# A gated mix of a state-space convolution and a mixer MLP on one core: the first mixer layer regrouped into three tiles of 128 channels and one of 64, with the gate's sums and some weight splits on other engines

## The chip, the cores and the metric

One core of a Trainium2 chip runs the whole program. The metric is the device time of one execution in microseconds (us): the median of three runs of the kernel before is 380.18 us (380.03 to 381.19). One further execution was recorded by the profiler; its own time is 380.4 us and its span, from the first to the last recorded instruction, is 378.6 us.

## What is computed

The reference mixes two branches of the same input x (2048 tokens, 448 channels). With L = 2048, D = 448, N = 256, F = 1792:

```python
x = A_u
g = _sigmoid((x * gate_w).sum(-1, keepdims=True))
a = _A_ref(x, ...)            # diagonal state-space convolution over L, plus u * D_skip
b = _B_ref(x, w1, w2, w3, w4)
return g * a + (1 - g) * b

def _B_ref(x, w1, w2, w3, w4):
    h = _gelu(_layernorm(x, axis=-1) @ w1)        # 448 -> 448, the first layer
    c = D // 4                                    # four channel groups of 112
    g0 = h[:, :, 0*c:1*c] shifted by +1 token     # (padded with zeros at the ends)
    g1 = h[:, :, 1*c:2*c] shifted by -1
    g2 = h[:, :, 2*c:3*c] shifted by +2
    g3 = h[:, :, 3*c:   ] shifted by -2
    hs = concatenate([g0, g1, g2, g3], -1) @ w2   # 448 -> 448, the second layer
    x1 = x + hs
    h2 = _gelu(_layernorm(x1, axis=-1) @ w3) @ w4 # 448 -> 1792 -> 448
    return x1 + h2
```

## The kernel before

**Precision.** Every float32 operand of a large matmul is split in two: a high part that TensorE takes exactly (type fp32r, written by ScalarE with a Copy) and a low part, the difference, written by VectorE. A product is then high·high + low·high + high·low: three matmuls for each tile. The input has 448 = 3·128 + 64 channels; the low part of the last 64 is stacked under their high part (`split_lo`, L360 to L365), so the contraction takes 4 + 4 + 3 = 11 matmuls of 512 columns for each output tile.

**Units.** The work of the mixer goes in units, `("a", b, i)` and then `("d", b, f)`. b is one of four blocks of 512 tokens. An a-unit is one channel group i of 112 of the first layer and its share of the second; the four groups are taken in the order 0, 2, 1, 3, so that unit n = 4b + 1 is group 2. A d-unit is one of 14 tiles of 128 of the 1792 hidden channels. There are 16 a-units (n = 0 to 15) and 56 d-units.

**One a-unit.** `first(n)` (L419, matmuls in L437) multiplies the block, read at the shifted token offset, by w1 (11 matmuls into one PSUM bank). `act_mul` (L440, VectorE) multiplies by the tokens' reciprocal standard deviations, which lie along the free axis in the row tile rb; they come from VectorE's and ScalarE's statistics, a Newton iteration (`rstd`, on VectorE in block 0 and 1, on GpSimd later: two instructions on VectorE, then 12 on GpSimd, L323 to L326), a TensorE transpose and a ScalarE copy (`rstd_rows`, L333). `act_head` (L448, ScalarE) applies the gelu (L456), `act_copy` (L466, ScalarE) writes the high part uh (L468), `act_tail` (L470, VectorE) the low part ul (L472), and `second(n)` (L482) multiplies uh and ul by w2: 3 products x 4 token tiles = 12 matmuls of 448 columns (L499). After a block's last group the sums are added to xs (L505).

**The order** is written by hand. `begin` (L805) lists block 0 by itself, with the splits of w1 and w2, the statistics and the warm-up matmuls. After that, one pass n of the main loop issues: work listed under `before` and `after` for n, `act_tail(n+1)`, `first(n+2)`, work under `between`, `act_head(n+2)`, `act_copy(n+2)`, `second(n)`. Each engine takes its instructions in that order, and waits at the front of its queue. The lists (`at(n, fn, ...)`, L905 on) hold the statistics, the splits of later inputs and weights (`split_xt`, `sp3`, `sp4`), the layer norm of the second stage (`norm_d`, `norm_turn`, `norm_hi`, `norm_lo`) and the convolution (`ssm_...`).

**The gate's logits** come from TensorE: the weight tiles of groups 0 and 1 have 114 columns, the last two of which hold gate_w, so two rows of the first layer's output are x·gate_w. `logits` (L537) copies them out with ScalarE (five times an instruction of 18 partitions x 512), a DMA writes them to memory, `logits_in` reads them back, and `gates` (L552) transposes them on TensorE and applies the sigmoid.

Names in the rows: p is the first layer's PSUM tile, rb the row of reciprocals, uf the scaled and then gelu'd tile, uh and ul its high and low parts, acc the second layer's sums, raw an input as loaded, xh and xl its parts, w1h/w1l to w4h/w4l the weights' parts. Lines of kernel.py:

Of the kernel before, what the change touches and what calls it, by code (L numbers as in the profile page):

```python
# [8 lines left out]
F32 = mybir.dt.float32  # L9
# [3 lines left out]
OP = mybir.AluOpType  # L13
# [11 lines left out]
GW = G + 2  # L25
# [4 lines left out]
SHIFT = (1, -1, 2, -2)  # L30
EPS = 1e-5
# [14 lines left out]
def gated_mix_kernel(tc, x, xT, xb, x0, w1, w2, w3, w4, par, logdt, dskip, ident, parg, uflip, lags, out):  # L46
    nc = tc.nc
    with tc.tile_pool(name="keep", bufs=1) as keep:
# [3 lines left out]
        with ExitStack() as ctx:  # L52
            mixer_and_small_steps(ctx, tc, xs, gg, okm, x, xT, xb, x0, w1, w2, w3, w4, par, logdt, dskip, ident, out)
# [121 lines left out]
def mixer_and_small_steps(ctx, tc, xs, gg, okm, x, xT, xb, x0, w1, w2, w3, w4, par, logdt, dskip, ident, out):  # L175
# [16 lines left out]
    lg = dr.tile([1, L + 2], F32, name="lg")  # L192
# [16 lines left out]
    nu = big.tile([128, 4, 4], F32, name="nu")  # L209

# [30 lines left out]

    w1h, w1l = wpair([128, 4, 4, GW], "w1")
    w2h, w2l = wpair([G, 4, D], "w2")
    w1r = big.tile([128, 4, 4, GW], F32, name="w1r", tag="w4al")
    w2r = big.tile([128, 4, D], F32, name="w2r", tag="w4ah")

    def first_loads():
# [5 lines left out]
        act(w1r[:, 0], w1[:, 0])  # L253
        sp(r[:, :2 * HW], x0[:, :2 * HW])
        act(w1r[:, 2], w1[:, 2])
# [3 lines left out]
        sp(w1r[:, 1], w1[:, 1])  # L259
# [3 lines left out]
        sp(w1r[:, 3], w1[:, 3])  # L263
# [6 lines left out]
    def constants():  # L270
# [7 lines left out]
        nc.gpsimd.memset(carry, 0.0)  # L278
        nc.gpsimd.memset(rb[:, 0:HALO], 0.0)
# [139 lines left out]
    def first(n, bank="p1", seq=None, stop=True):  # L419
# [3 lines left out]
        if kind == "a":  # L423
            m = GW if i < 2 else G
            wh, wl = w1h[:, i, :, :m], w1l[:, i, :, :m]
            o = HALO - SHIFT[i]
        else:
            m = 128
            wh, wl = (w[:, :, i * m:(i + 1) * m] for w in (w3h, w3l))
            o = 0  # L430
# [4 lines left out]
        every = [(w, x_, k, 0, TB) for w, x_, r in ((0, 0, 4), (1, 0, 4), (0, 1, 3)) for k in range(r)]  # L435
        for q, (w, x_, k, t0, t1) in enumerate(seq or every):
            nc.tensor.matmul(p[:m, t0:t1], (wl if w else wh)[:, k, :], (xl if x_ else xh)[:, k, o + t0:o + t1],  # L437
                             start=(q == 0 and fresh), stop=stop if q + 1 == len(seq or every) else False)

    def act_mul(n):  # L440

        kind, b, i = units[n]
        m = G if kind == "a" else 128
        UF[n] = wk.tile([128, TB], F32, name="uf")
        o = b * TB + HALO - SHIFT[i]
        nc.vector.tensor_mul(UF[n][:m], P1[n][:m], rb[:m, o:o + TB])  # L446

    def act_head(n, later=False):  # L448
        kind, b, i = units[n]
        m = G if kind == "a" else 128  # L450
# [597 lines left out]
```

## Time and profile before

| | |
|---|---|
| median of three runs | 380.18 us |
| profiled execution, own time | 380.4 us |
| its span | 378.6 us |
| TensorE busy | 368.5 us, 1713 matmuls |
| VectorE busy | 295.8 us |
| ScalarE busy | 210.2 us |
| GpSimd busy | 71.1 us |

A profile's page gives the busy time of each engine, the chain that ended last and the groups of instructions. In the rows PE is TensorE, DVE VectorE, ACT ScalarE, POOL GpSimd. A row of a timeline has the start, the duration, engine, line, operation, output<-inputs, shape, count and, in brackets, how long the engine had been idle and what released it. Instructions of an engine overlap a little: two 512-column operations of VectorE start 0.60 us apart and each lasts 0.69 us.

### The profile page before, as it was taken

Reading aid. Unit: us, or ns where it says so; the run is one execution under the profiler, and the core shown is the slowest. Engines: PE = TensorE matmul, PEld = TensorE weight load, DVE = VectorE, ACT = ScalarE, POOL = GpSimd, SP = SyncE. Lnnn points to the kernel's source line nnn. Section 1 sums busy time; section 2 is a strip of 40 time slices with the busy share of each in tenths; the row PEclk is TensorE's granted clock in tenths of the full one; section 3 lists DMA queues with packets and bytes.
Section 4 is the critical chain, followed back from the end, with each engine's and each line's share of the span. In section 5 each row is a group of like instructions: output and inputs, shape, how many; then the busy total and the mean of one; then the engine's idle time right before and its main releaser. Section 6 shows DMA issues by size and latency. Waiting matters only on the chain.

```text
span 378.6 us, 5180 instructions
## 1 busy us (share of the span) xinstructions
PE 368.5 (97%) x1713; PEld 314.6 (83%) x1713; DVE 295.8 (78%) x527; ACT 210.2 (56%) x349; POOL 71.1 (19%) x187
## 2 busy tenths in 40 slices
PE   7998999999999999999999999999999999999993
PEld 4786888888888888888888888888888888888883
DVE  4888979785858981998399989999787999996312
ACT  4764646546978467643465575465756654442220
POOL 3200070322000000040023536324041440000000
PEclk9999999999999999999999999999999999999998
DMA  8970606166615219000843515256685311372202
GB/s 266 397 265 1 224 1 173 30 118 209 209 56 157 46 50 214 3 0 12 243 72 78 83 29 153 63 160 124 97 183 134 78 28 19 73 189 48 77 0 102
DMA packets 85896, 42.26 MB, mean 112 GB/s; under 512 B 67030, under 2 KB 80614, under 8 KB 85226
## 3 DMA queue, kind: packets, MB, share of 16 engines
q1 hardware_dynamic: 85434, 41.20, 41.6%
q10 hardware_dynamic: 432, 0.70, 0.6%
q8 instruction: 15, 0.25, 0.3%
q14 instruction: 15, 0.12, 0.1%
HBM read 30.86 MB, written 11.02 MB: 111 GB/s over the span
## 4 chain that ended last, share of the span: by engine, by line
PE 90%; DVE 3%; ACT 2%; DMA 2%; issue 1%; POOL 0%; SPq 0%; DVEq 0%
PE p L437 46%; PE acc L499 43%; DMA w1r<-w_in 2%; PE acc L520 1%; ACT uh L468 1%; ACT uf L456 1%; PE misc L336 0%; DVE uf L446 0%; DVE z L638 0%; DVE w2l L218 0%; DVE b L286 0%; ACT w2h L217 0%; ACT xn L294 0%; DVE ul L472 0%; DVE xh L365 0%
## 5 line engine op out<-in xcount | busy, mean ns | idle before, releaser
L459 ACT ACTIVATE uf<-p 128x512 f32<-128x512 f32 x56 | 33.4, 597 | 101.9 <-PE p L437 101.8
L472 DVE TENSOR_TENSOR ul<-uf,uh 128x512 fp32r<-128x512 f32 (+1 forms) x72 | 48.9, 680 | 31.5 <-ACT uh L468 31.4
L638 DVE TENSOR_TENSOR_SCAN z<-z,carry 128x512 f32<-128x512 f32 x48 | 61.5, 1281 | 4.6 <-ACT z L633 0.7
L437 PE MATMUL p<-xh,w3h 128*128 128x512 f32 x224 | 61.3, 396 | 0.0
L437 PE MATMUL p<-xh,w3l 128*128 128x512 f32 x224 | 60.7, 392 | 0.0
L499 PE MATMUL acc<-w4h,uh 128*128 128x448 f32 x216 | 55.8, 364 | 0.3 <-DVE xs L508 0.3
L499 PE MATMUL acc<-w4h,ul 128*128 128x448 f32 x216 | 55.7, 364 | 0.0
L499 PE MATMUL acc<-w4l,uh 128*128 128x448 f32 x216 | 55.7, 363 | 0.0
L437 PEld LDWEIGHTS p<-xh,w3l 128*128 128x128 f32 x224 | 42.1, 188 | 9.9
L437 PE MATMUL p<-xl,w3h 128*128 128x512 f32 x168 | 48.0, 394 | 0.0
L437 PEld LDWEIGHTS p<-xh,w3h 128*128 128x128 f32 x224 | 42.0, 188 | 6.7
L468 ACT ACTIVATE uh<-uf 128x512 fp32r<-128x512 f32 (+1 forms) x72 | 45.6, 633 | 2.3
L499 PEld LDWEIGHTS acc<-w4h,uh 128*128 128x128 f32 x216 | 40.5, 188 | 6.6 <-issue 0.7
L499 PEld LDWEIGHTS acc<-w4l,uh 128*128 128x128 f32 x216 | 40.5, 188 | 3.1
L499 PEld LDWEIGHTS acc<-w4h,ul 128*128 128x128 f32 x216 | 40.5, 188 | 2.9
L633 ACT ACTIVATE z<-zs,nu 128x512 f32<-128x512 f32 x64 | 42.2, 710 | 0.8 <-DMA zs<-xT_in 0.4
L632 POOL COPY z<-carry 128x1 f32<-128x1 f32 x48 | 34.6, 731 | 17.4 <-DVE zs L644 17.1
L437 PEld LDWEIGHTS p<-xl,w3h 128*128 128x128 f32 x168 | 31.5, 188 | 7.2
L323 POOL TENSOR_TENSOR t<-r 128x4 f32<-128x4 f32 (+1 forms) x15 | 6.8, 453 | 133.2 <-DVE r L321 132.5
L640 POOL COPY carry<-z 128x1 f32<-128x1 f32 x48 | 14.1, 294 | 92.4 <-DVE z L638 91.5
L456 ACT ACTIVATE uf<-uf 112x512 f32<-112x512 f32 x16 | 10.1, 630 | 24.2 <-DVE uf L446 24.1
L638 DVE TENSOR_TENSOR_SCAN z<-z,carry,zero 128x512 f32<-128x512 f32 x16 | 20.0, 1247 | 0.0
(150 smaller groups left out, 496.5 us busy)
## 6 DMA issues: line engine op xcount, KB each, us to landing
zs<-xT_in SPq DMA_DIRECT2D x4, 1024.0 KB, 8.1
yd<-yt SPq DMA_DIRECT2D x56, 64.0 KB, 2.0
ysb<-yd SPq DMA_DIRECT2D x16, 224.0 KB, 3.0
out_dram<-xs SPq DMA_DIRECT2D x16, 224.0 KB, 2.8
raw<-xb_in SPq DMA_DIRECT2D x3, 1032.0 KB, 7.9
raw<-w_in SPq DMA_DIRECT2D x3, 1024.0 KB, 5.6
xd<-xt SPq DMA_DIRECT2D x16, 192.0 KB, 2.1
xr<-xd SPq DMA_DIRECT2D x16, 192.0 KB, 3.5
```

Source lines behind the costliest of these rows:

```text
L323: eng.tensor_mul(t, y, y)
L437: nc.tensor.matmul(p[:m, t0:t1], (wl if w else wh)[:, k, :], (xl if x_ else xh)[:, k, o + t0:o + t1], start=(q == 0 and fresh), stop=stop ...
L456: nc.scalar.activation(UF[n][:m], UF[n][:m], AF.Gelu_apprx_tanh)
L459: nc.scalar.activation(UF[n][:m], P1[n][:m], AF.Gelu_apprx_tanh)
L468: nc.scalar.activation(UH[n][:m], UF[n][:m], AF.Copy)
L472: nc.vector.tensor_sub(UL[n][:m], UF.pop(n)[:m], f32(UH[n][:m]))
L499: nc.tensor.matmul(ACC[j], (UL if p == 2 else UH)[n][:m, t], wl if p == 1 else wh, start=s and p == 0, stop=e and p == 2)
L520: nc.tensor.matmul(ACC[j], (UL if p == 2 else UH)[m][:, t], wl if p == 1 else wh, start=False, stop=m > n and p == 2)
L632: nc.gpsimd.tensor_copy(z4[:, m, 0:1], carry[:, k, m:m + 1])
L633: nc.scalar.activation(z4[:, m, 1:], ZS[b][:, k, :], AF.Copy, scale=nu[:, k, m:m + 1])
L638: nc.vector.tensor_tensor_scan(z, z, up, carry[:, k, m:m + 1], OP.add, OP.add)
L640: nc.gpsimd.tensor_copy(carry[:, k, m:m + 1], z[:, TB - 1:])
```

## The change

**Groups.** Group 2 is split: 64 of its 112 channels stay a unit (GD = 64, unit n = 4b + 1), and 16 go to each of the three other groups, which become tiles of 128 (GX = 16). The 64-channel unit has its high weights in columns 0 to 63 of the tile w1d and the low ones in columns 64 to 127, so that 4 + 3 = 7 matmuls replace 11; `act_add` (ScalarE copies the lower half of the PSUM tile, VectorE adds it to the upper) joins the two. In the second layer its uh holds the high part in partitions 0 to 63 and the low part in 64 to 127, w2 holds the same rows twice, and 8 matmuls replace 12.

**Shifts.** The 16 foreign channels of a 128-tile need group 2's token shift, not the tile's. `act_mul` writes the scaled tile behind four spare columns; GpSimd copies the last four columns of the previous block into them from the tile skew (L472) and saves its own last four (L475). ScalarE applies the gelu to the whole tile (L488) and once more to the 16 rows at the other offset (L489), which waits for the copy. `first_tokens` computes, with four small matmuls, the first one or two tokens of these 16 rows for groups 1 and 3 in block 0, which those tiles' own windows lack.

**Gate.** The extra columns, `logits` and `logits_in` are gone. gate_w is loaded as a 128 x 448 tile (`gate_load`); for each of the 16 token tiles GpSimd multiplies it with x (`gate_mul`, 128 x 448) and ScalarE sums (`gate_sum`, a Copy with an accumulator).

**Splits.** The low parts of w1's groups 1 and 3 and of w2's groups 2, 1 and 3 are taken by GpSimd. In `begin` the order is written anew: three of block 1's four high splits come later, four warm-up matmuls (`keep_warm`) are gone, and `second(3)` is issued in two pieces around `rstd_rows`.

The diff, cut:

```diff
+GX = 128 - G
+GD = G - 3 * GX
+SKEW = 4
...
-    w1h, w1l = wpair([128, 4, 4, GW], "w1")
-    w2h, w2l = wpair([G, 4, D], "w2")
+    w1h, w1l = wpair([128, 3, 4, 128], "w1")
+    w1d = big.tile([128, 4, 128], F32R, name="w1d", tag="w4bh")
+    w2h, w2l = wpair([128, 4, D], "w2")
...
         if kind == "a":
-            m = GW if i < 2 else G
-            wh, wl = w1h[:, i, :, :m], w1l[:, i, :, :m]
+            wh, wl = (w1d, None) if i == 2 else (w1h[:, TI[i]], w1l[:, TI[i]])
...
+    def act_add(n):
+        p = P1[n]
+        UF[n] = wk.tile([128, TB], F32, name="uf")
+        nc.scalar.activation(UF[n][:GD], p[GD:], AF.Copy)
+        nc.vector.tensor_add(UF[n][:GD], p[:GD], UF[n][:GD])
...
     def act_mul(n):
...
+        UF[n] = wk.tile([128, SKEW + TB], F32, name="uf")
+        nc.gpsimd.tensor_copy(UF[n][:GX, :SKEW], skew[:, TI[i], :])
+        nc.vector.tensor_mul(UF[n][:, SKEW:], p, rb[:, o:o + TB])
+        if b + 1 < NB:
+            nc.gpsimd.tensor_copy(skew[:, TI[i], :], UF[n][:GX, TB:])
...
+            o = SKEW - (SHIFT[2] - SHIFT[i])
+            uf, UF[n] = UF[n], big.tile([128, TB], F32, name="ug", tag="w4bl")
+            nc.scalar.activation(UF[n], uf[:, SKEW:], AF.Gelu_apprx_tanh)
+            nc.scalar.activation(UF[n][:GX], uf[:GX, o:o + TB], AF.Gelu_apprx_tanh)
...
-        if kind == "a" and n and (i == 0 or (i == 1 and b == NB - 1)):
-            logits(p, b, i)
...
+        if kind == "a" and i == 2:
+            nc.vector.tensor_sub(UH[n][GD:], uf[:GD], f32(UH[n])[:GD])
...
-        q = [(j, p) for p in range(3) for j in range(NT)]
+        q = [(j, p) for p in range(2 if kind == "a" and i == 2 else 3) for j in range(NT)]
...
+    def gate_mul(j):
+        GP[j] = wk.tile([128, 512], F32, name="gp", tag="u")
+        nc.gpsimd.tensor_mul(GP[j][:, :D], xs[:, j, :], GR[0])
+
+    def gate_sum(j):
+        t = GP.pop(j)[:, :D]
+        nc.scalar.activation(t, t, AF.Copy, accum_out=gg[:, j:j + 1])
...
     def gates():
-        p = ps.tile([128, L // 128], F32, name="misc", bufs=1)
-        nc.tensor.transpose(p, LT[0], idt[:L // 128, :L // 128])
-        nc.scalar.activation(gg, p, AF.Sigmoid)
+        nc.scalar.activation(gg, gg, AF.Sigmoid)
...
         first(4)
         rstd(r1, NT + 1, 2 * NT + 1)
+        gate_load()
...
+        for j in range(NT):
+            gate_mul(j)
+            gate_sum(j)
         first(5)
+        act_add(5)
+        second(3, slice(0, 6))
         rstd_rows(NT + 1, 2 * NT + 1)
         stats_b(2 * NT + 1, 2 * NT + 3)
         act_head(4)
         act_head(5)
         act_tail(4)
-        second(3)
+        second(3, slice(6, None))
...
-    at(13, logits_in)
+    for j, n in zip(range(NT, L // 128), (4, 4, 5, 6, 7, 7, 8, 9, 11, 12, 13, 14)):
+        at(n - 1 if n > 4 else n, gate_mul, j)
+        at(n, gate_sum, j, when=between)
```

**Three places in the order.** ScalarE at the end of `begin`, from the last statistics (L293 and L294 before, L307 and L308 after) to the high part of unit 4. Before:

```order
L293 ACTIVATE xn_371,st_81<-xs_58 128x448
L294 ACTIVATE xn_371,st_81<-xs_58,st_81 128x448
L337 ACTIVATE rb_75<-misc_435 128x512
L456 ACTIVATE uf_448<-uf_448 112x512
L468 ACTIVATE uh_447<-uf_448 112x512
```

and in the changed kernel, where L587 is `gate_sum`, the first L456 the copy of `act_add(5)`, and L351 the row rb:

```order
L307 ACTIVATE xn_385,st_80<-xs_58 128x448
L308 ACTIVATE xn_385,st_80<-xs_58,st_80 128x448
L587 ACTIVATE gp_439,gg_59<-gp_439 128x448
L587 ACTIVATE gp_442,gg_59<-gp_442 128x448
L587 ACTIVATE gp_445,gg_59<-gp_445 128x448
L587 ACTIVATE gp_448,gg_59<-gp_448 128x448
L456 ACTIVATE uf_459<-p1_451 64x512
L351 ACTIVATE rb_75<-misc_468 128x512
L488 ACTIVATE ug_485<-uf_479 128x512
L489 ACTIVATE ug_485<-uf_479 16x512
L503 ACTIVATE uh_483<-ug_485 128x512
```

Five instructions now stand between the statistics and rb, and one more between the gelu and uh.

VectorE at the same place, from the last step of the Newton iteration (L310, L324) to ul of unit 4. Before:

```order
L310 SCALAR_TENSOR_TENSOR r1_82<-t_405,r1_82 128x4
L286 BN_STATS b6_441<-xs_58 128x6 x2
L288 BN_AGGR st_81<-b6_441 128x2 x2
L446 TENSOR_TENSOR uf_448<-p1_392,rb_75 112x512
L446 TENSOR_TENSOR uf_457<-p1_423,rb_75 112x512
L472 TENSOR_TENSOR ul_446<-uf_448,uh_447 112x512
```

and after, where L457 is the addition of `act_add(5)`:

```order
L324 SCALAR_TENSOR_TENSOR r1_81<-t_419,r1_81 128x4
L457 TENSOR_TENSOR uf_459<-p1_451,uf_459 64x512
L300 BN_STATS b6_474<-xs_58 128x6 x2
L302 BN_AGGR st_80<-b6_474 128x2 x2
L473 TENSOR_TENSOR uf_479<-p1_406,rb_75 128x512
L469 TENSOR_TENSOR uf_459<-uf_459,rb_75 64x512
L511 TENSOR_TENSOR ul_484<-ug_485,uh_483 128x512
```

The addition, which needs ScalarE's copy L456, has come ahead of the statistics and of unit 4's multiplication.

GpSimd in block 1, from the end of the Newton iteration that follows the statistics of pass 5. Before, nothing but the next iteration follows:

```order
L326 TENSOR_TENSOR r1_82<-r1_82,t_531 128x4
L323 TENSOR_TENSOR t_590<-r2_83 128x4
L324 TENSOR_TENSOR t_590<-t_590,v_589 128x4
L325 TENSOR_SCALAR t_590<-t_590 128x4
L326 TENSOR_TENSOR r2_83<-r2_83,t_590 128x4
```

In the changed kernel the copies for units 7 and 8 (L472 into uf_607 and uf_690) and the gate's products (L583) share that queue. The end of the first iteration, the copy for unit 7 and the start of the second iteration:

```order
L340 TENSOR_TENSOR r1_81<-r1_81,t_569 128x4
L583 TENSOR_TENSOR gp_584<-xs_58,gr_431 128x448
L472 COPY uf_607<-skew_94 16x4
L475 COPY skew_94<-uf_607 16x4
L337 TENSOR_TENSOR t_631<-r2_82 128x4
```

and the second iteration's end with the copy for unit 8:

```order
L340 TENSOR_TENSOR r2_82<-r2_82,t_631 128x4
L344 TENSOR_SCALAR nm_77<-st_80 128x4
L345 TENSOR_TENSOR nm_77<-nm_77,r2_82 128x4
L583 TENSOR_TENSOR gp_648<-xs_58,gr_431 128x448
L583 TENSOR_TENSOR gp_650<-xs_58,gr_431 128x448
L472 COPY uf_690<-skew_94 16x4
```

Each copy, for which unit 7's and unit 8's second gelu waits, now stands behind 12 or 14 instructions of an iteration and one or two products.

204 lines of the change are left out of this document (119 added, 85 removed).

## The prediction

> **What bounds the kernel now.** I read the page first: busy time by engine, and the shares of the chain that ended last.
>
> ```profile
> PE 368.5 (97%) x1713; PEld 314.6 (83%) x1713; DVE 295.8 (78%) x527; ACT 210.2 (56%) x349; POOL 71.1 (19%) x187
> PE 90%; DVE 3%; ACT 2%; DMA 2%; issue 1%; POOL 0%; SPq 0%; DVEq 0%
> ```
>
> TensorE is the bound over the whole span. The chain in order of time gives its pieces; of the units that change, the first in the dense stretch (unit 4) and the last (unit 15):
>
> ```profile
> 38.30 2.53 PE p L437 x11
> 40.82 2.41 PE acc L499 x12
> ...
> 96.55 2.41 PE acc L499 x12
> ```
>
> A first layer takes 2.53/11 = 0.230 us a matmul, a second 2.41/12 = 0.201 us. From 35.23 us on these pieces follow one another without a gap, so a microsecond less on TensorE is a microsecond less of span, as long as the others keep up. Whether they do is read from the busy time in the three blocks of a-units behind block 0:
>
> ```profile
> 38.30:58.60 20.30, 20.30 (x97) 17.14 (x97) 17.13 (x38) 11.86 (x21) 7.08 (x26) 1.00 0.34 114
> 58.60:78.80 20.20, 20.20 (x96) 17.04 (x96) 16.62 (x35) 10.83 (x18) 3.90 (x12) 1.00 0.38 100
> 78.80:98.96 20.16, 20.16 (x94) 17.06 (x93) 14.12 (x26) 13.16 (x19) 4.70 (x14) 1.00 0.63 173
> ```
>
> Columns: length, PE, weight loads, DVE, ACT, POOL, clock. VectorE is busy 84% of the first block, and it and ScalarE hand one tile back and forth. How close they run shows at the end, on VectorE:
>
> ```profile
> 38.61 0.69 DVE L472 TENSOR_TENSOR ul<-uf,uh 112x512 fp32r<-112x512 f32 x1 [0.76 <-ACT uh L468]
> ...
> 95.62 1.29 DVE L472 TENSOR_TENSOR ul<-uf,uh 112x512 fp32r<-112x512 f32 x2
> ```
>
> The first row is ul of unit 4. The second holds ul of units 15 and 16; unit 15's ends at about 96.30, and its second layer, begun at 96.55, needs it in its third matmul, at 96.95. **TensorE is ahead of the other chain by only 0.65 us there.** The second chain is nearly a bound already; I price the change on both.
>
> **TensorE.** The order holds seven and eight matmuls for units 1, 5, 9 and 13, so the change does what it says. Each loses 4 x 0.230 = 0.92 us in the first layer and 4 x 0.201 = 0.80 us in the second, 1.72 us a block, 6.9 us in all. Block 0's share lies in a stretch where other engines end last (waits below), which leaves 3 x 1.72 = 5.2 us. One of unit 5's halves, its first layer, is in that stretch too: 4.3 us. The logits' transpose goes (0.16 us), and wider tiles cost nothing: the column count of the moving operand stays. TensorE's own path would so reach unit 15 4.4 us earlier.
>
> **The start.** TensorE's longest wait between its first matmul and the end is for the row of reciprocals of block 1, as the list of waits has it:
>
> ```profile
> PE misc L336 <- DVE r L310: 1.1, 1, 1.1
> ```
>
> and the timelines of ScalarE and VectorE around it:
>
> ```profile
> 27.26 0.63 ACT L456 ACTIVATE uf<-uf 112x512 f32<-112x512 f32 x1 [2.14 <-DVE uf L446]
> ...
> 31.54 0.19 ACT L294 ACTIVATION_READ_ACCUMULATOR xn<-xs,st 128x1 f32 x1
> 35.92 0.60 ACT L337 ACTIVATE rb<-misc 128x512 f32<-128x512 f32 x1 [4.19 <-PE misc L336]
> ...
> 35.09 1.15 DVE L286 BATCH_NORM_STATS2 b<-xs 128x6 f32<-128x448 f32 x2
> 36.16 0.30 DVE L288 BATCH_NORM_AGGREGATE st<-b 128x2 f32<-128x6 f32 x2
> 36.55 1.29 DVE L446 TENSOR_TENSOR uf<-p,rb 112x512 f32<-112x512 f32 x2
> ```
>
> ScalarE is idle for 4.19 us ahead of rb. The order fills that hole with four gate sums and a copy. The prices, from groups of like shape (a sum is L293 with its accumulator read; the second gelu on 16 rows is like the logits' copy of 18 rows, since time goes by columns):
>
> ```profile
> L293 ACT ACTIVATE xn<-xs 128x448 f32<-128x448 f32 x4 | 2.3, 566 | 0.8 <-DMA xs<-x_in 0.8
> L293 ACT ACTIVATION_READ_ACCUMULATOR xn<-xs 128x1 f32 x4 | 0.7, 186 | 0.0
> L540 ACT ACTIVATE lr<-p 18x512 f32<-18x512 f32 x5 | 3.0, 592 | 0.1
> L446 DVE TENSOR_TENSOR uf<-p,rb 112x512 f32<-112x512 f32 x16 | 10.9, 686 | 3.4 <-ACT rb L337 3.1
> L729 POOL TENSOR_TENSOR wsum<-w1r 128x112 f32<-128x112 f32 x3 | 1.2, 384 | 7.0 <-DMA w1r<-w_in 7.0
> L730 POOL TENSOR_TENSOR wsum<-wsum,w1r 128x112 f32<-128x112 f32 x3 | 1.7, 561 | 0.2
> L324 POOL TENSOR_TENSOR t<-t,v 128x4 f32<-128x4 f32 x12 | 2.4, 200 | 0.9
> ```
>
> A GpSimd product of 448 columns is not in the trace. Between 4 and 112 columns the rows rise by 184 ns, 1.7 ns a column; so 0.95 us (an estimate), bounded by 0.38 us (the 112-column row) and 1.7 us (the slope to L730's 561 ns). I take 0.95, on the line of the two undisturbed rows. [...]
>
> ScalarE reaches the end of its statistics 0.6 to 1.5 us later than at 31.73: three second gelus (3 x 0.66) and two more splits of block 1 (1.1) come in, 0.7 us goes in a wait for a low w2 part on GpSimd, 2.1 us of idle time there is used up; unit 0 starts up to 1 us earlier, because unit 1's shorter first layer brings rb forward. Four sums at the pace of GpSimd's products take 3.5 us, the copy 0.6: it ends 4.1 us behind the statistics. VectorE then adds (0.60), does the two statistics ahead of unit 4 (1.4) and multiplies: at 38.4 to 39.3 against 36.55. With unit 4's second gelu (0.66), ul of unit 4 is 2.5 to 3.4 us late: **+3.0**. Unit 5's shorter layer doesn't help, since TensorE waits.
>
> **The chain in blocks 1 to 3.** Between a multiplication and ul, VectorE has other work, which hides ScalarE's gelu and uh. Unit 6:
>
> ```profile
> 44.60 0.69 DVE L446 TENSOR_TENSOR uf<-p,rb 112x512 f32<-112x512 f32 x1
> ...
> 45.99 0.63 ACT L468 ACTIVATE uh<-uf 112x512 fp32r<-112x512 f32 x1
> ...
> 46.81 0.17 DVE L321 TENSOR_SCALAR r<-v 128x4 int32<-128x4 int32 x1
> 46.89 0.68 DVE L472 TENSOR_TENSOR ul<-uf,uh 112x512 fp32r<-112x512 f32 x1
> ```
>
> uh is there at 46.62; ul starts at 46.89 when its cover ends. A second gelu of 0.66 shows 0.4 of it. Units 6, 7 and 10 have this cover (0.4 each). Units 11 and 15 have none, since VectorE waits for ScalarE work that follows their uh (first and last row below), 0.66 each. In 8, 12 and 14 the second gelu takes the place of the logits' copy, and 4 is counted above. Sum **+2.6**.
>
> ```profile
> 70.12 0.56 DVE L373 TENSOR_TENSOR xl<-xr,xh 128x384 fp32r<-128x384 f32 x1 [1.88 <-ACT xh L406]
> ...
> 54.32 0.69 DVE L446 TENSOR_TENSOR uf<-p,rb 112x512 f32<-112x512 f32 x1 [1.41 <-ACT rb L337]
> ...
> 93.48 1.23 DVE L218 TENSOR_TENSOR w3l<-raw,w3h 128x1024 fp32r<-128x1024 f32 x1 [2.31 <-ACT w3h L217]
> ```
>
> The additions of units 9 and 13 put 0.60 each on VectorE: **+1.2**. A gate sum ahead of w3's split costs 0.7. The wait of 1.41 for rb (middle row) was set by TensorE; with TensorE's part no longer last it shrinks, to about 0.4 by my count of ScalarE's queue: together **-0.3**.
>
> **GpSimd's queue.** The second gelu waits for the copy L472, and that stands behind Newton iterations and products. The iterations as they run now, and the gelus of units 7 and 14 beside them:
>
> ```profile
> 47.06 0.57 POOL L323 TENSOR_TENSOR t<-r 128x4 f32<-128x4 f32 x1 [33.70 <-DVE r L321]
> ...
> 50.51 0.20 POOL L326 TENSOR_TENSOR r<-r,t 128x4 f32<-128x4 f32 x1
> 51.19 1.78 POOL L323 TENSOR_TENSOR t<-r 128x4 f32<-128x4 f32 x1 [0.48 <-DVE r L321]
> ...
> 49.46 0.63 ACT L456 ACTIVATE uf<-uf 112x512 f32<-112x512 f32 x1 [2.84 <-DVE uf L446]
> ...
> 82.06 0.17 DVE L321 TENSOR_SCALAR r<-v 128x4 int32<-128x4 int32 x1
> ...
> 84.59 0.63 ACT L456 ACTIVATE uf<-uf 112x512 f32<-112x512 f32 x1 [3.96 <-DVE uf L446]
> ...
> 82.31 1.71 POOL L323 TENSOR_TENSOR t<-r 128x4 f32<-128x4 f32 x1 [11.57 <-DVE r L321]
> ...
> 87.77 0.22 POOL L331 TENSOR_TENSOR nm<-nm,r 128x4 f32<-128x4 f32 x1
> ```
>
> One takes 3.7 us (47.06 to 50.71); one with the two nm instructions 5.7 (82.31 to 87.99), some 4.2 without the 1.5 us that its first instruction stood still. GpSimd's copies have no row of this shape; I take 0.25, a little above L324's 0.20; up to 0.38 (L729) it would add 0.1 a wait. Unit 7: iteration 3.7, product 0.95, copy 0.25, ready 4.9 us after VectorE's L321, which ends at 46.98. The gelu ends at 50.09, 3.1 later, 3.5 with unit 6's later ul between. ScalarE waits 1.4. Unit 8: behind unit 7's copy stand the other iteration (3.9), two products (1.9) and two copies (0.5): 6.3; ScalarE and VectorE need 5.1 for the rest of unit 7, two splits, a sum, rb, multiplication and gelu: 1.2. Unit 14: 4.2 + 0.95 + 0.25 = 5.4 after L321 (82.23), while the gelu ends 3.0 after it (85.22): 2.4. Behind the waiting gelu stand uh, unit 7's splits and rb, and for those VectorE waits, then TensorE. Sum **+5.0**.
>
> **Other edits, taken at nothing.** The low w1 and w2 parts on GpSimd end before TensorE asks, but for the 0.7 us above; with 1.7 us products they would cost 1 us more. Loads of w1 are 44 KB less before group 1's, the gate's 229 KB lands while ScalarE splits. The warm-up matmuls ran in a wait.
>
> **Sum.** 3.0 + 2.6 + 1.2 - 0.3 + 5.0 = 11.5, less the 0.65 of room: unit 15 starts 10.9 us later, and from there TensorE has its old work. Span 378.6 + 10.9 = 389.5; own time 380.4 + 10.9 = **391.3 us**. The profiled execution lies 0.2 us above the median; I leave it so. With the product at 0.38 us the waits fall to 2.7 and the start by 0.8: 388. At 1.7 us both rise, by 3 and 1.5: 396.
>
> **Rivals.**
>
> 1. *The saving comes through* (0.22): faster, 380.4 - 4.4 = 376.0 us. For it: TensorE is 97% busy and ScalarE has 44% idle, GpSimd 81%. It decides at unit 15: ul must be there by 92.6, 3.7 us sooner than now, through a chain that got longer. Only if most of the added work falls into idle time does it happen.
>
> 2. *GpSimd's queue doesn't hold the gelus* (0.23): the 5.0 us go, the rest stays: 386.3 us. For it: copies are small and products may be shorter than my estimate; against it: the order.
>
> 3. *Products stop VectorE as well* (0.05, with all above 395). In the trace L324 takes 200 ns alone, while the first instructions of two iterations took 1.78 and 1.71 us beside VectorE's subtractions: one engine stood still for the other. If each of 12 products holds a VectorE subtraction by half its length and two thirds count: 12 x 0.48 x 0.67 = 3.8 us, 395 us. [...]
>
> 4. *A slower TensorE clock in the new gaps* (in the 0.05 as well). The first matmuls, on an idle TensorE, took longer:
>
> ```profile
> 1.31 3.44 PE L764 MATMUL pw<-warm 128*128 128x512 bf16 x8 [1.31 <-POOL cm L273]
> ```
>
> 0.43 us each, against 0.230. If three gaps made 3.4 us of work half as fast, 3 x 1.7 = 5.1 us: 396. [...]
>
> 5. *No change* (0.06): the two sides cancel within 0.3%, about what a measurement of this kernel can tell from no change.
>
> **How the numbers follow.** My forecast (387.5 to 395) 0.44; rival 2 (381.6 to 387.5) 0.23; above 395, 0.05; together slower 0.72. Same 0.06. Faster 0.22. The range 376 to 395 leaves out about half of the faster case and the top: under 2 in 10.
>
> **What would show it.** TensorE's matmul count falls by some 30; idle time of PE in 35 to 115 us released by ul and uh; ScalarE's L489 waiting for GpSimd's L472, 1 to 3 us at units 7, 8 and 14; rb of block 1 near 37 us; GpSimd's L583 near 0.95 us. If ul of unit 15 ends before 95, the chain was misread and rival 1 holds. If L489 never waits, rival 2.

## The result, and the profile after

The changed kernel takes 409.8 us (median of 4 runs, 408.7 to 410.3), the kernel before 380.5 us beside it: 1.076 times as long (95% interval 1.073 to 1.080). The profiled execution's own time is 408.7 us, its span 406.9 us. The direction was forecast; the size was not: 28.3 us more span, where 10.9 were worked out, and the time lies far above the range.

From the page after, busy time by engine and the chain that ended last by engine:

```profile
PE 375.3 (92%) x1684; PEld 316.2 (78%) x1684; DVE 306.0 (75%) x529; ACT 225.8 (55%) x392; POOL 102.1 (25%) x235
PE 73%; DVE 10%; ACT 5%; DMA 5%; POOL 4%; issue 3%; ACTq 0%; SPq 0%; DVEq 0%; POOLq 0%
```

TensorE's matmuls fell by 29, as planned, and its share of the chain fell from 90% to 73%: for a quarter of the span something else ends last. The list of TensorE's waits (us in total, times, longest) says where:

```profile
PE acc L537 <- ACT uf L483: 10.3, 2, 5.3
PE misc L350 <- DVE r L324: 2.8, 1, 2.8
PE p L450 <- ACT xh L420: 2.7, 1, 2.7
PE acc L537 <- DVE ul L511: 2.6, 1, 2.6
PE misc L350 <- POOL r L340: 1.4, 1, 1.4
```

The two waits of 5 us stand ahead of the second layers of units 8 and 12, the first units of blocks 2 and 3; the 2.8 us stand ahead of rb of block 1. (The list names the work that ended last before the wait did. L483 is the gelu of the next unit, of which these layers read nothing; what they need are the PSUM banks that VectorE's additions to xs set free.) A first layer of the d-units, the second of them (unit 17), starts at 93.73 us before and at 121.36 after, and from there both kernels need the same time to the end (284.9 and 285.5 us). So the whole loss lies in the a-units. On VectorE, ul of unit 4 ends 5.8 us later than before (45.07 against 39.30), that of unit 8 10.4 later, of unit 12 22.7, of unit 14 27.0.

Three things in this stretch deserve a look before the experiments. First, **the second 5 us wait.** These are VectorE, GpSimd and ScalarE ahead of it, in three fences:

```profile
92.34 0.67 DVE L473 TENSOR_TENSOR uf<-p,rb 128x512 f32<-128x512 f32 x1
96.27 0.65 DVE L403 STREAM_TRANSPOSE xt<-xn 128x448 f32<-128x448 f32 x1 [3.26 <-ACT gp L587]
99.26 0.65 DVE L403 STREAM_TRANSPOSE xt<-xn 128x448 f32<-128x448 f32 x1 [2.34 <-DMA xd<-xt]
...
101.10 0.68 DVE L469 TENSOR_TENSOR uf<-uf,rb 64x512 f32<-64x512 f32 x1
101.71 2.20 DVE L543 TENSOR_TENSOR xs<-acc,xs 128x448 f32<-128x448 f32 x4
```

```profile
86.38 1.16 POOL L583 TENSOR_TENSOR gp<-xs,gr 128x448 f32<-128x448 f32 x1
...
87.62 1.15 POOL L583 TENSOR_TENSOR gp<-xs,gr 128x448 f32<-128x448 f32 x1
```

```profile
95.59 0.56 ACT L587 ACTIVATE gp<-gp 128x448 f32<-128x448 f32 x1
96.05 0.19 ACT L587 ACTIVATION_READ_ACCUMULATOR gp<-gp 128x1 f32 x1
101.82 0.63 ACT L483 ACTIVATE uf<-uf 64x512 f32<-64x512 f32 x1 [5.58 <-DVE uf L469]
102.48 0.63 ACT L501 ACTIVATE uh<-uf 64x512 fp32r<-64x512 f32 x1
103.02 0.56 ACT L587 ACTIVATE gp<-gp 128x448 f32<-128x448 f32 x1
```

The transposes of the layer norm (`norm_turn`) write a tile xt that is taken from tag u, which has two buffers. The change takes its products gp from the same tag. Two products, made at 86.38 and 87.62, fill both buffers; the first is summed at 95.59, the second at 103.02. So the first transpose waits for a sum of ScalarE, and the second one has the same buffer to itself only after the first one's DMA has read it, 2.34 us later. VectorE stands at the front of its queue for 5.6 us in all, and behind it stand ul of unit 12, the multiplication of unit 13, for which ScalarE waits 5.58 us, and the additions to xs, for which TensorE's next block waits: the first of the four ends at 102.32, TensorE's wait at 102.47. It happens at both of block 0's pairs: the group of these four transposes stands for 8.7 us, where none of them waits in the kernel before. But the first pair, at 73.28 and 76.21, comes behind the first 5 us wait (until 71.00) and can't have made it. Ahead of that one, unit 8's second gelu waits 2.40 us for GpSimd, and a multiplication of VectorE takes 1.50 us instead of 0.68 beside a product.

Second, **small VectorE instructions beside products** at the end of `begin`, VectorE and then GpSimd:

```profile
32.82 1.61 DVE L511 TENSOR_TENSOR ul<-ug,uh 128x512 fp32r<-128x512 f32 x1
34.35 1.12 DVE L315 TENSOR_SCALAR v<-st 128x4 f32<-128x4 f32 x1
35.50 1.08 DVE L317 TENSOR_SCALAR r<-v 128x4 int32<-128x4 int32 x1
36.62 1.04 DVE L320 TENSOR_TENSOR t<-r 128x4 f32<-128x4 f32 x1
37.69 0.16 DVE L322 SCALAR_TENSOR_TENSOR t<-t,v 128x4 f32<-128x4 f32 x1
```

```profile
32.72 4.92 POOL L583 TENSOR_TENSOR gp<-xs,gr 128x448 f32<-128x448 f32 x4
37.58 0.18 POOL L472 COPY uf<-skew 16x4 f32<-16x4 f32 x1
```

Four products in a row, four VectorE instructions in a row that last about 0.9 us longer than they need (ul takes 0.69 and each of the others 0.17 us where no product runs); with the last product they are short again.

Third, **the clock.** TensorE's windows of 10 us (busy times of PE, PEld, DVE, ACT, POOL; the granted clock is the third number from the end):

```profile
70.00:80.00 10.00, 8.81 (x34) 7.44 (x35) 6.77 (x12) 3.45 (x8) 1.57 (x3) 0.83 0.27 63
90.00:100.00 10.00, 6.26 (x21) 5.10 (x21) 4.34 (x11) 4.67 (x9) 0.00 (x0) 0.83 0.08 23
100.00:110.00 10.00, 7.53 (x23) 6.50 (x24) 8.01 (x16) 3.40 (x6) 3.50 (x11) 0.66 0.72 172
```

Behind each of the five longest waits the clock falls: to 0.83 and 0.66 in the windows behind the two of 5 us, to 0.83 in 90 to 100 us behind the 2.6 us for ul, and, in windows not printed here, to 0.84 in 40 to 50 behind the 2.8 us for rb and 0.83 in 110 to 120 behind the 2.7 us for xh. The second layer of unit 12 (102.47 to 107.08) takes 4.6 us instead of 2.41.

### The profile page after: what moved, and what is told of

Same layout as the page of the kernel before. It is cut to its first block, busy times and chain, and to the rows that moved or that the text cites. A ratio compares the mean times of both kernels' runs of the same rounds, so it can differ in the third digit from the quotient of the medians.

```text
span 406.9 us, 5254 instructions
## 1 busy us (share of the span) xinstructions
PE 375.3 (92%) x1684; PEld 316.2 (78%) x1684; DVE 306.0 (75%) x529; ACT 225.8 (55%) x392; POOL 102.1 (25%) x235
## 4 chain that ended last, share of the span: by engine, by line
PE 73%; DVE 10%; ACT 5%; DMA 5%; POOL 4%; issue 3%; ACTq 0%; SPq 0%; DVEq 0%; POOLq 0%
PE p L450 37%; PE acc L537 35%; DMA w1r<-w_in 3%; DVE b L300 2%; DMA raw<-w_in 1%; DVE xl L377 1%; PE acc L558 1%; DVE xs L543 1%; ACT ug L489 1%; POOL t L339 1%; DVE uf L473 1%; POOL gp L583 1%; DVE xh L379 1%; ACT uh L503 1%; ACT ug L488 1%
## 5 line engine op out<-in xcount | busy, mean ns | idle before, releaser
L450 PE MATMUL p<-xh,w3l 128*128 128x512 f32 x224 | 61.9, 399 | 0.0
L511 DVE TENSOR_TENSOR ul<-uf,uh 128x512 fp32r<-128x512 f32 x56 | 38.0, 678 | 28.2 <-ACT uh L503 28.1
L667 POOL COPY z<-carry 128x1 f32<-128x1 f32 x48 | 35.6, 753 | 17.2 <-DVE zs L679 17.1
L503 ACT ACTIVATE uh<-uf 128x512 fp32r<-128x512 f32 x56 | 35.5, 633 | 1.8
L537 PE MATMUL acc<-w2h,uh 128*128 128x448 f32 x64 | 22.3, 417 | 13.3 <-ACT uf L483 10.3
L337 POOL TENSOR_TENSOR t<-r 128x4 f32<-128x4 f32 (+1 forms) x15 | 3.5, 230 | 100.5 <-DVE r L335 99.7
L537 PEld LDWEIGHTS acc<-w2h,uh 128*128 128x128 f32 x64 | 13.3, 212 | 17.3 <-issue 6.0
```

What stands on the lines that cost most here:

```text
L450: nc.tensor.matmul(p[:, t0:t1], (wl if w else wh)[:, k, :], (xl if x_ else xh)[:, k, o + t0:o + t1], start=(q == 0 and fresh), stop=stop i ...
L503: nc.scalar.activation(UH[n], UF[n], AF.Copy)
L511: nc.vector.tensor_sub(UL[n], uf, f32(UH[n]))
L537: nc.tensor.matmul(ACC[j], (UL if p == 2 else UH)[n][:, t], wl if p == 1 else wh, start=s and p == 0, stop=e and p == 2)
L667: nc.gpsimd.tensor_copy(z4[:, m, 0:1], carry[:, k, m:m + 1])
```

## The experiments

My theory: the shared buffers, GpSimd's products holding VectorE, and the second gelus waiting for GpSimd make the loss. Rivals: ScalarE's added work itself; the slower clock; the splits on GpSimd. All runs are timed against the kernel before on the same chip (380.0 to 380.5 us there):

| run | median, us | ratio to before, 95% |
|---|---|---|
| the changed kernel | 409.8 | 1.073 to 1.080 |
| e1_own_buffer | 401.3 | 1.052 to 1.056 |
| e2_sum_only | 393.7 | 1.034 to 1.037 |
| e3_gelu_no_copy | 406.3 | 1.066 to 1.069 |
| e4_no_gate | 391.9 | 1.027 to 1.033 |
| e5_no_gate_no_copy | 386.7 | 1.015 to 1.020 |
| e6_splits_vector | 412.6 | 1.081 to 1.087 |
| e7_clock_filled | 409.6 | 1.074 to 1.079 |
| e8_gate_vector | 396.5 | 1.041 to 1.048 |
| e9_before_fewer_matmuls | 380.4 | 0.999 to 1.003 |
| e10_no_gate_one_gelu | 381.1 | 1.001 to 1.004 |
| e11_vector_gate_two_piece | 393.5 | 1.033 to 1.038 |
| e12_own_buffer_no_copy | 397.1 | 1.044 to 1.048 |
| e13_sums_apart | 401.3 | 1.054 to 1.059 |
| e14_copies_for_products | 394.7 | 1.035 to 1.040 |
| e15_clock_filled_2 | 409.5 | 1.074 to 1.079 |

### Own buffers for the transposes

```diff
 def norm_turn(b, i):
-    t = wk.tile([128, 512], F32, name="xt", tag="u")
+    if b == 0:
+        if not XT:
+            XT.append(big.tile([128, 4, D], F32, name="xt0", tag="w4al"))
+        t = XT[0][:, i]
+    else:
+        t = wk.tile([128, 512], F32, name="xt", tag="u")
```

(The tile of w4 with that tag is claimed later, when it is first written.)

> The four transposes of block 0 get buffers of their own; the gate's products keep the two of tag u for themselves. Theory (products held the transposes' buffers, VectorE stood behind them 8.7 us, TensorE waited twice for 5 us and its clock fell): the waits of xt in L403 go, the two long TensorE waits at the second layers of units 9 and 13 shrink below 2 us, the time falls by 10 to 15 us to 395 to 400 us. Rival (the chain is longer anyway by ScalarE's sums, the second gelus and the waits for GpSimd's copies, and the transposes only stood where VectorE would have waited for something else): within 3 us of 409.8.

Measured: 401.3 us, **8.5 us less**, just short of the theory's 10, and well beyond the rival's 3. The second pair of transposes now is one row without a wait, on VectorE:

```profile
88.79 0.67 DVE L478 TENSOR_TENSOR uf<-p,rb 128x512 f32<-128x512 f32 x1
89.38 1.16 DVE L408 STREAM_TRANSPOSE xt<-xn 128x448 f32<-128x448 f32 x2
91.54 0.69 DVE L516 TENSOR_TENSOR ul<-ug,uh 128x512 fp32r<-128x512 f32 x1 [1.00 <-ACT uh L508]
```

ul of unit 12 ends at 92.23 instead of 100.48. One thing of the theory was wrong: TensorE still waits 7.1 us at the two block starts (10.3 in the changed kernel). The wait of 5.3 us ahead of unit 8 is untouched, and the wait ahead of the d-units' first layer has grown from 2.7 to 5.2 us. The waits are where the late chain shows, and the buffers were one of several things that made it late.

### Sums without products, no gate at all

```diff
 def gate_mul(j):
-    GP[j] = wk.tile([128, 512], F32, name="gp", tag="u")
-    nc.gpsimd.tensor_mul(GP[j][:, :D], xs[:, j, :], GR[0])
+    pass
 def gate_sum(j):
-    t = GP.pop(j)[:, :D]
-    nc.scalar.activation(t, t, AF.Copy, accum_out=gg[:, j:j + 1])
+    nc.scalar.activation(GR[0], xs[:, j, :], AF.Copy, accum_out=gg[:, j:j + 1])   # e2; e4: pass
```

> The products on GpSimd are left out; ScalarE sums x itself, so the gate's values are not those of the reference. ScalarE's work is the same, GpSimd's 16 products and their buffers are gone. Theory (buffers, GpSimd's queue and VectorE held beside products): 12 to 22 us less than the changed kernel, 388 to 398 us. Rival (the 16 sums and the second gelus on ScalarE are what lengthens the chain): at most 5 us less, 405 to 410 us.

> Products and sums are left out, the gate is constant. What is left of the change is the regrouping, the second gelus with their copies, the additions and the splits on GpSimd. Theory (the gate's path is most of the loss): 383 to 391 us, and 2 to 6 us under the kernel that keeps the sums. Rival (the regrouped tiles themselves cost it, by second gelus, additions and low parts on GpSimd): 396 us or more.

Measured: 393.7 and 391.9 us. Sixteen sums on ScalarE cost 1.8 us, a little less than the 2 to 6 expected; the products cost 16.1, of which 8.5 were the buffers. The rest of the change still costs 11.5 us (391.9 against 380.4 beside it): e4 came out just above the theory's 391, so the gate is most of the loss and not all.

### What the products do to VectorE

e2 leaves open whether products hold VectorE or only make ScalarE's sums wait. In e13 the products stay and the sums read x and wait for none:

```diff
-    nc.scalar.activation(t, t, AF.Copy, accum_out=gg[:, j:j + 1])
+    if not JK:
+        JK.append(big.tile([128, 4 * D], F32, name="jk", tag="w4ah"))
+    nc.scalar.activation(JK[0][:, :D] if j < 14 else t, xs[:, j, :], AF.Copy, accum_out=gg[:, j:j + 1])
```

e14 is e13 with `nc.gpsimd.tensor_copy(GP[j][:, :D], xs[:, j, :])` for the product, so it forms no product either.

> Transposes with buffers of their own, GpSimd's products as in the changed kernel, but ScalarE sums x itself (the last two products aside) and waits for no product; the gate's values are not those of the reference. Theory (products hold VectorE): as with own buffers, 399 to 402 us. Rival (ScalarE's sums waiting for products made the loss): as without products, 393 to 396 us.

> The same, with a GpSimd copy of 128x448 (one input) in the place of each product (two inputs). If only instructions of two inputs hold VectorE: 393 to 395 us, and VectorE's small operations at 34 us take 0.17 us each. If any GpSimd instruction of this width does: 396 to 400 us, by its length.

Measured: 401.3 us, the same as e1, and 394.7 us, one above e2. So **7.6 us are products holding VectorE**, and none is a sum waiting. VectorE's groups between 28 and 120 us (busy us, mean ns of one) show which instructions are held. e13:

```profile
L516 DVE TENSOR_TENSOR ul<-ug,uh 128x512 fp32r<-128x512 f32 x10 | 10.4, 1044 | 8.2 <-ACT uh L508 8.2
L300 DVE BATCH_NORM_STATS2 b<-xs 128x6 f32<-128x448 f32 x17 | 9.7, 611 | 0.0
...
L315 DVE TENSOR_SCALAR v<-st 128x4 f32<-128x4 f32 x1 | 1.1, 1125 | 0.0
```

and e2, without products:

```profile
L300 DVE BATCH_NORM_STATS2 b<-xs 128x6 f32<-128x448 f32 x17 | 9.7, 611 | 0.0
...
L511 DVE TENSOR_TENSOR ul<-ug,uh 128x512 fp32r<-128x512 f32 x10 | 6.9, 688 | 6.1 <-ACT uh L503 6.1
...
L315 DVE TENSOR_SCALAR v<-st 128x4 f32<-128x4 f32 x1 | 0.2, 170 | 0.8 <-ACT xn L308 0.8
```

The low part ul, with both inputs in SBUF, takes 1044 ns instead of 688 on average. A tensor_scalar of four columns, with one input, takes 1125 ns instead of 170; a product takes 1168 ns on average in e13. The statistics with one input are as fast as ever (611 ns in both runs), but only one of the 17 ran beside a product (at 57.30, 0.38 of its 0.61 us). The multiplication uf<-p,rb, with one input in PSUM, never ran beside one here, so its time says nothing about a hold. The additions to xs, also with one input in PSUM, did so in the changed kernel, VectorE and then GpSimd:

```profile
70.24 2.20 DVE L543 TENSOR_TENSOR xs<-acc,xs 128x448 f32<-128x448 f32 x4
```

```profile
68.64 2.67 POOL L583 TENSOR_TENSOR gp<-xs,gr 128x448 f32<-128x448 f32 x2 [2.34 <-ACT gp L587]
```

Two of the four run while the products last, and the four take 2.20 us, as they do at 101.71 without a product. VectorE's busy time is 305.7 us in e13 against 298.6 in e2, 7.1 more for the same instructions, about what the time lost. So ul and the tensor_scalar are held, the additions and the one row of statistics are not. What sets the tensor_scalar, with its one input, apart from the statistics no row shows.

A copy on GpSimd holds VectorE too, but for less. VectorE and GpSimd in e14, at the place that was shown above:

```profile
33.98 0.49 DVE L315 TENSOR_SCALAR v<-st 128x4 f32<-128x4 f32 x1 [0.46 <-ACT xn L308]
34.50 0.47 DVE L317 TENSOR_SCALAR r<-v 128x4 int32<-128x4 int32 x1
35.01 0.16 DVE L320 TENSOR_TENSOR t<-r 128x4 f32<-128x4 f32 x1
```

```profile
32.41 2.53 POOL L591 COPY gp<-xs 128x448 f32<-128x448 f32 x4
```

A copy takes some 0.6 us and holds a tensor_scalar for 0.3 us; a product takes 1.2 and holds it for 0.9. The expectation's "0.17 us each" was wrong, its time right.

### The second gelu: its wait and its own time

```diff
-            nc.scalar.activation(UF[n][:GX], uf[:GX, o:o + TB], AF.Gelu_apprx_tanh)
+            nc.scalar.activation(UF[n][:GX], uf[:GX, SKEW:], AF.Gelu_apprx_tanh)   # e3, e5, e12; e10: the line goes
```

> The second gelu reads the tile's own columns without the shift, so it no longer needs GpSimd's copy; the copies stay, the 16 foreign channels come out with the wrong token. Theory (five gelus stand 8.2 us behind GpSimd's queue and the chain pays most of it): 5 to 9 us less, 401 to 405 us. Rival (what follows a waiting gelu is late for another reason, the buffers or VectorE): at most 2 us less, 408 to 410 us.

> The gate is left out as in the run without it (391.9 us), and the second gelu reads the tile's own columns, so that it waits for no copy; the foreign channels come out with the wrong token. In the trace without the gate L490 waits 0.98, 1.37, 0.81 and 2.21 us for the copies. Theory (these waits are on the chain of VectorE and ScalarE, which is the bound): 387 to 390 us, 2 to 5 us less than without the gate. Rival (the rest of the loss is in VectorE's order, the additions and low parts, and the waits fall beside it): 391 to 392 us.

> The changed kernel without the gate and without the second gelu, so the 16 foreign channels of a tile keep the tile's own shift; the copies on GpSimd stay and nobody waits for them. Against the run with the second gelu but without its wait (386.7 us): theory (the second gelu's own time is exposed by 0.4 to 0.66 us a unit as the prediction has it): 3 to 5 us less, 382 to 384 us. Rival (it is hidden behind VectorE's work): within 1 us of 386.7.

> The changed kernel with buffers of their own for the transposes (401.3 us) and a second gelu that waits for no copy (foreign channels with the wrong token); products and sums stay. What is left of the products is what they do to VectorE. Without a gate the same kernel took 386.7 us. Theory (buffers and queue waits were nearly all): 388 to 391 us. Rival (products hold VectorE, which is busy 7 us more beside them than without): 393 to 397 us.

In the changed kernel the second gelu waits 8.2 us for GpSimd in five waits, 1.23 of it at unit 7, 2.40 at unit 8, 3.35 at unit 14 and 0.98 at unit 3, and it runs 0.63 us twelve times; its line's row:

```profile
L489 ACT ACTIVATE ug<-uf x12: 628/630/632, 21.0 to 119.0; 16x512 f32<-16x512 f32 x12
its engine sat idle before it (us, times) until:
  POOL uf L472: 8.2, 5
```

Taking the wait away saves 3.5 us in the changed kernel (e3, between theory and rival), 4.2 with own buffers (e1 to e12) and 5.2 without the gate (e4 to e5): part of it hides behind the other losses as long as these are there. e12 lies at the upper end of the rival's range (393 to 397): with buffers and queue waits gone, the products still stand for most of the 10.4 us above e5. Taking the gelu itself away saves **5.6 us** more (e5 to e10), of 12 x 0.63 = 7.6 us that it runs, and more than the 3 to 5 us expected. At e10 the change, without its gate and without the shift of 16 channels, is 1.0 us slower than the kernel before.

### Is TensorE's saving worth anything?

The kernel before, with the low parts of group 2's weights left out:

```diff
+        if kind == "a" and i == 2:
+            seq = [s_ for s_ in seq or every if not s_[0]]
...
-        q = [(j, p) for p in range(3) for j in range(NT)]
+        q = [(j, p) for p in ((0, 2) if kind == "a" and i == 2 else range(3)) for j in range(NT)]
```

> The kernel before, in which units 1, 5, 9 and 13 leave out the low parts of their weights: 7 matmuls instead of 11 and 8 instead of 12, as many as the change saves, and nothing else is touched. Theory (VectorE and ScalarE end only 0.65 us behind TensorE, so TensorE's saving has nothing to shorten): 379 to 380.4 us. Rival (TensorE is the bound and its 4.4 to 5.2 us come through): 375 to 376 us.

Measured: 380.4 us, no difference. From its page and its list of TensorE's waits:

```profile
PE 364.3 (96%) x1681; PEld 309.7 (82%) x1681; DVE 295.5 (78%) x527; ACT 209.9 (56%) x349; POOL 70.0 (19%) x187
```

```profile
PE misc L336 <- DVE r L310: 2.1, 1, 2.1
PE p L439 <- ACT xh L406: 1.7, 1, 1.7
```

TensorE has 32 matmuls and 4.2 us of work less, and waits nearly as much longer: 1.0 us more for rb, 1.7 for xh, the rest in small pieces. **An engine that is busy 97% of the span was not the only bound in the blocks that the change touches.** One thing this run doesn't separate: behind the longer wait for rb the clock falls, and the twelve matmuls there take 4.1 us (35.26 to 39.35) instead of 2.41. Over the ten runs the time goes with the mean granted clock, from 378.7 us at 0.998 to 381.6 at 0.986. So 1 to 2 us of the saving may have been lost to the clock; the 375 to 376 us of the rival were reached in none of them.

### The clock

Dummy matmuls into the idle bank misc ahead of TensorE's waits, in e7 ahead of `rstd_rows` of block 1 and of the second layers of units 9, 12 and 13, in e15 ahead of those of units 8 and 12 (24 each) and of unit 16's first layer (12):

```diff
+            if n in FILL:
+                keep_warm(FILL[n], n // 4)
             if n < len(units) - 2:
                 second(n)
```

> The whole changed kernel, with dummy matmuls of 512 columns into the idle bank misc ahead of four waits of TensorE: 10 ahead of the row rb of block 1, 20 ahead of the second layers of units 9 and 13, 9 ahead of that of unit 12. In the changed kernel's trace twelve matmuls after these gaps take 3.7 to 4.6 us instead of 2.41. Theory (the slower clock behind a gap lengthens the path): granted clock 1.00 in the windows 40 to 110 us, 4 to 8 us less, 402 to 406 us. Rival (TensorE's slow matmuls run while it would wait anyway): within 1.5 us of 409.8, or a little longer by the dummies.

> The whole changed kernel, with 24 dummy matmuls each ahead of the second layers of units 8 and 12, where TensorE waits 5.3 and 5.0 us, and 12 ahead of unit 16's first layer (a wait of 2.7 us). Theory (slow matmuls behind the first two gaps run while VectorE is late anyway; only the last gap's 2 us are on the path): 407.5 to 410 us, with the granted clock at 1.00 in 70 to 80 and 100 to 120 us. Rival (the clock costs what the rows show, 1.6 + 2.7 + 2.0 us): 402 to 405 us.

e7 left the first of the two long waits as it was, since its dummies for units 9 and 13 stood one unit too late, behind the waits; the nine ahead of unit 12 filled 2.2 us of the second wait and left 3.8, behind which the clock fell again. e15 hit both:

```profile
70.00:80.00 10.00, 8.56 (x39) 7.07 (x39) 6.75 (x12) 3.45 (x8) 1.59 (x3) 1.00 0.26 61
90.00:100.00 10.00, 8.69 (x32) 7.33 (x33) 4.35 (x11) 4.77 (x9) 0.00 (x0) 0.83 0.08 23
100.00:110.00 10.00, 10.00 (x47) 8.61 (x47) 8.11 (x17) 3.41 (x6) 3.46 (x10) 1.00 0.77 187
```

Measured: 409.6 and 409.5 us, nothing gained. The slow matmuls ran in time that TensorE had anyway, since VectorE was late. In e15 the clock stayed at 0.83 in 90 to 100 us, behind a wait of 2.57 us that no dummy filled, and at 0.83 in 110 to 120, where twelve were too few and 2.17 us of the wait were left; in e7 it was 1.00 in both of these windows, and low (0.94, 0.72 and 0.83) only in 60 to 70, 70 to 80 and 100 to 110, where e15 has 1.00; that run took the same time. No run had it at 1.00 throughout, and none filled the gaps of a kernel without the other losses, so this holds for the changed kernel as it stands.

### Splits, and the gate on VectorE

```diff
-        lo_(*s2(2), nc.gpsimd)
+        lo_(*s2(2))          # e6: so for all five
```

> The whole changed kernel, with the five low parts of w1 and w2 back on VectorE. Theory (the splits on GpSimd cost block 0 little, as the prediction took them at nothing): within 2 us of 409.8. Rival (they hold VectorE's subtractions, 1.54 us instead of 0.69 beside one of them, and make w2's low parts late): 3 to 6 us less, 404 to 407 us. A third way: five more instructions of VectorE make block 0 longer, 411 to 413 us.

Measured: 412.6 us, the third way: the five splits on GpSimd save 2.8 us. e8 does product and sum in one VectorE instruction (has e1's buffers, and in `begin` sums behind the gelus of units 4 and 5); e11 also replaces copy and second gelu by two pieces, one of which reads the saved columns:

```diff
+        nc.vector.scalar_tensor_tensor(t[:, :D], xs[:, j, :], 1.0, GR[0], op0=OP.mult, op1=OP.mult,
+                                       accum_out=gg[:, j:j + 1])
...
+            nc.scalar.activation(UF[n][:GX, SKEW - o:], uf[:GX, SKEW:o + TB], AF.Gelu_apprx_tanh)
+            nc.scalar.activation(UF[n][:GX, :SKEW - o], skew[:, TI[i], o:], AF.Gelu_apprx_tanh)
```

> Product and sum of the gate in one instruction of VectorE with an accumulator (16 of some 0.6 us), the transposes of block 0 in buffers of their own; GpSimd and ScalarE do nothing for the gate. Theory (the waits were the gate's cost, VectorE has idle time behind ScalarE's gelus to hide most of 9.6 us): 391 to 395 us, at most 3 us above the kernel without a gate. Rival (VectorE is the bound of these blocks, and every instruction on it counts): 397 to 402 us.

> The gate on VectorE and the transposes in buffers of their own (396.5 us), and the second gelu in two pieces that read the tile and the saved columns directly, so that no copy of GpSimd stands ahead of it; some 0.2 us more of ScalarE each. Theory (the waits for the copies, 5 us in the run without the gate): 391 to 393 us. Rival (the additional piece eats the gain, or VectorE's 16 instructions are the bound now): 395 us or more.

Measured: 396.5 and 393.5 us. Sixteen VectorE instructions of 0.615 us cost 4.6 of their 9.8 us, between theory and rival; the copy's waits gave 3.0 back, which ends just above the theory's 393. e11 leaves nothing out and is 16 us faster than the change, and still 13 slower than the kernel before. Since even e10, which leaves out the gate and the shift, does not beat that kernel, I tried no further version on this order of work.

## Why the prediction was wrong

The runs form a ladder from the kernel before to the change. Each step is one term (medians, about 1 us uncertain; taken in another order a step can differ, as the second gelu's wait does). The forecast's terms are sorted into the same steps; how its start and its additions divide between the second and the fifth row is my estimate.

| step | forecast, us | measured, us |
|---|---|---|
| TensorE's saving, beyond the room of 0.65 | 0 | 0 (e9) |
| regrouping, additions, copies of `act_add`, splits | about 0.9 | 1.0 (e10) |
| second gelus' own time | 3.3 | 5.6 (e10 to e5) |
| second gelus waiting for GpSimd | 5.0 | 5.2 (e5 to e4) |
| 16 sums on ScalarE | about 1.7 | 1.8 (e4 to e2) |
| products holding VectorE | 0 | 7.6 (e2 to e1, e13) |
| products in the transposes' buffers | 0 | 8.5 (e1 to the change) |
| sum | 10.9 | 29.7 (29.3 when timed side by side) |

- **TensorE's units lose 1.72 us a block, and it is worth nothing but 0.65.** Right: 29 matmuls fewer, no time gained. Rival 1 (376.0) fell, and e9 shows that it would have fallen even if the rest of the change had cost nothing. (The room itself was read a little too wide: unit 15's third matmul, the first that needs ul, starts at 96.79 in the timeline and not at 96.95, which leaves 0.5.)
- **The start, +3.0.** Right without the products: ul of unit 4 ends 3.4 us late in e2, and VectorE waits there for ScalarE's copy, as forecast. That is partly luck, since the sums take 2.8 us there, at their own pace, and not the products' 3.5. With the products it is 5.8, by another path: rb comes at 40.01 instead of near 37, because four VectorE instructions ahead of it stood 0.9 us each.
- **The chain in blocks 1 to 3, +2.6.** The mechanism was right, the size too small: 5.6 for all twelve units instead of 3.3 with unit 4's (2.6 is a slip besides; its terms add up to 2.5). I had let VectorE's other work hide 0.2 to 0.3 us of units 6, 7 and 10, and counted nothing in the units where the gelu takes the place of the logits' copy; e10 shows three quarters of a gelu on average.
- **GpSimd's queue, +5.0, and 1.4, 1.2 and 2.4 us at units 7, 8 and 14.** Right in mechanism: 1.23, 2.40 and 3.35 in the trace. That the sum came out too, 5.2 us in time, is partly luck: the waits of the changed kernel add up to 8.2 us, and taking them away gains 3.5 us there and 5.2 only without the gate. Rival 2 fell. The product took 1.12 to 1.16 us undisturbed, where I had put 0.95.
- **Rival 3, products stop VectorE (0.05, 3.8 us).** It happened, at twice the price. The evidence stood in the forecast (a GpSimd instruction of 1.78 us beside VectorE's subtractions, where others like it take 0.20), yet the sum carried zero for it. This is the first failed step: in a stretch where VectorE is busy 84%, a hold was treated as an unlikely extra, and the runs show 7.6 us.
- **"Other edits, taken at nothing".** The splits on GpSimd cost nothing and save 2.8 us (e6), which the second row of the ladder already holds; the loads no run tested. But the products' tile was an edit too, and its tag was in the diff: `tag="u"`, which `norm_turn` and `wsum` use. I priced instructions and queues and didn't ask who else takes turns in that buffer. This is the second failed step and the largest missing term, 8.5 us.
- **Rival 4, the clock.** It fell, to 0.66 in one window of 10 us, as that rival said. No run shows its three stretches of 3.4 us at half pace as such: the kernel before has its first matmuls (3.44 us, 0.43 us each), and in the changed kernel the matmuls of a second layer take 0.37 us instead of 0.20, for about 3 us behind the first 5 us wait (71.00 to 74.03) and for more than 4.6 behind the second. In the changed kernel it cost nothing that these runs could see (e7, e15), because it fell where TensorE had time; in e9 a cost of 1 to 2 us stays open.

The marks named in the forecast did appear: 29 fewer matmuls, waits for ul and uh, L489 waiting at units 7, 8 and 14. They were true of a kernel that lost 11 us and of one that lost 28; only the marks on rb (37 against 40.01) and on the product (0.95 against 1.15) gave a part of the difference away.

## What to carry to other kernels

For every new tile read its tag: who else rotates through these buffers, and how long does the slowest user hold one? For everything moved to GpSimd, list VectorE's instructions beside it and price the hold. Here a product of 1.2 us held ul, which reads two SBUF inputs, and a tensor_scalar for 0.9 us each, a copy of 0.6 us held them for 0.3, and the additions to xs, with one input in PSUM, took the same 2.20 us for four beside products as without. And before an engine's saving is counted, take the saving alone (as e9 does, by leaving work out): if that gains nothing, a change that has no other gain can only cost.

## What was not expected of the hardware

The clock did not fall by the length of a gap alone. Ahead of rb of block 1 TensorE waits 2.78 us in the changed kernel and 2.77 in e15, at the same place of the span; behind it the granted clock is 0.84 in the one, here,

```profile
40.00:50.00 10.00, 9.47 (x37) 7.87 (x37) 8.49 (x14) 6.86 (x14) 4.46 (x5) 0.84 0.00 1
```

and 1.00 in e15:

```profile
40.00:50.00 10.00, 7.90 (x37) 6.55 (x37) 8.49 (x14) 6.86 (x14) 4.47 (x5) 1.00 0.00 1
```

In e4 the clock fell behind a gap of 2.05 us (0.83 in 60 to 70 us):

```profile
63.46 0.45 PE L538 MATMUL acc<-w2h,uh 128*128 128x448 f32 x1 [2.05 <-ACT uf L484]
...
64.14 0.41 PE L538 MATMUL acc<-w2h,uh 128*128 128x448 f32 x1
64.35 0.57 PE L538 MATMUL acc<-w2l,uh 128*128 128x448 f32 x1
64.72 0.57 PE L538 MATMUL acc<-w2h,ul 128*128 128x448 f32 x1
```

Its first matmuls run at full pace, and 0.9 us behind the gap each takes 0.37 us instead of 0.20. In e15 a wait of 2.10 us, ahead of 45.82, left the matmuls at 0.20. So about the same length goes with a lower clock in one run and with the full one in another; what else decides it, these traces do not show.

And three VectorE instructions of four columns took 1.04 to 1.12 us each beside GpSimd's products, longer than one of 512 columns takes alone (0.69); the four products beside them took 4.92 us.
